# Six matmuls into a spare PSUM tile between the last output projection and the third piece of w4, in a decode kernel on one core

## The chip, the cores and the metric

The kernel runs on one core of one Trainium2 chip. The metric is the device time in microseconds. Executions of one kernel mostly agree within 0.3%; each comparison below is made on one chip, against executions of the kernel before in the same rounds. Times within a trace count from the start of its span.

In the profiles, PE is the engine for matmuls, PEld its weight loads, DVE and ACT are the vector and scalar engines, and SP is the engine that issues the loads; a "q" behind a name is that engine's sequencer. PSUM is the memory that matmuls write to. "Landing" is the moment at which a load has arrived. The granted clock is the share of its full clock that PE was given. Score matmuls are those of q k^T, PV matmuls those of p v; a V tile is the load of V that one head needs. Only some lines of each view are shown.

## The reference, cut to what matters

The reference adds two branches to its input: attention of one new token over the last 2048 entries of a K and V cache (4 batches, 32 query heads, 16 KV heads, head size 128), and a small MLP.

```
xn  = layernorm(x)                         # x: 4 x 1 x 576
q   = xn @ wq                              # 576 x 4096
p   = softmax(q k^T / sqrt(128))           # over the last 2048 positions
a   = (p v) @ wo                           # 4096 x 576
...                                        # layernorm; for S=1 the shifted part adds zero
h2  = gelu(layernorm(x1) @ w3) @ w4        # 576 x 4608, 4608 x 576
out = x + a + x1 + h2
```

Nearly all bytes are K and V (67 MB); w4 is 5.3 MB. All that is summed into the output is accumulated in PSUM, at the end in two tiles that are then added.

## The kernel before

The loads stand in one queue: K and V tiles in turn, wo in four parts, w3, and last w4 in six pieces. SP issues each when its buffer comes free. PE transposes and multiplies behind them. Only the tail matters here. `acc` and `acc_odd` are two PSUM tiles; their matmuls have 8 output rows each, in different column groups of the array, and two of them run side by side: in the trace of before the two of a pair start within 0.01 us of each other, and the pairs follow at 0.12 us. `mlp_out` multiplies rows of w4, `o_proj` rows of wo; a "row" in this text is one of the 36 blocks of 128 rows of w4.

```python
W4_PIECES = [0, 10, NFH, NF - 6, NF - 2, NF - 1, NF]     # 0, 10, 18, 30, 34, 35, 36

def load_w4():
    t = wp.tile([P, NF, D], BF16, tag="w", name="w4_sb")
    for lo, hi in zip(W4_PIECES, W4_PIECES[1:]):
        ...
        nc.sync.dma_start(out=t[:, lo:hi, :], in_=src[...])
...
def mlp_out(lo, hi):
    w4 = w_tiles["w4"]
    for i in range(lo, hi, 2):
        acc_matmuls([(gT[:, u, :], w4[:, u, :]) for u in range(i, min(i + 2, hi))])
...
mlp_out(*pieces[0])
o_turn(hl)                  # transposes, DVE sums, spreading: the last heads' attention
o_sum(hl)
o_spread(hl)
o_pick(hl)
mlp_out(*pieces[1])
o_proj(hl)                  # the last output projection, 16 matmuls
mlp_out(*pieces[2])         # the third piece of w4: rows 18 to 29
mlp_out(*pieces[3])
second.clear()              # from here all into acc
odd = const.tile([OR, CW], F32)
nc.scalar.activation(out=odd[:], in_=acc_odd[QD:QD + OR, :], func=ACT.Copy)
...
for lo, hi in pieces[4:]:   # the last two rows
    mlp_out(lo, hi)
fin = ...                   # acc + odd, to the output
```

## Time and profile before

| what | value |
|---|---|
| median of 3 executions, then of 6 | 211.7 us, 211.75 us (211.63 to 211.93) |
| span of the trace | 209.8 us |
| PE, DVE, ACT busy | 71%, 57%, 16% |
| DMA | 87.32 MB, of them 87.17 by the main queue; mean 416 GB/s |

These lines are from the page of before: the granted TensorE clock and the busy share of the DMA engines in 40 slices, in tenths, then the shares of the chain of waits by engine.

```profile
PEclk9999589696997556958999979997999985969999
DMA  8999999999999999999999999999999999999991
DMA 73%; PE 17%; DVE 7%; ACT 1%; issue 1%; SPq 0%; DVEq 0%
```

DMA is busy from end to end.

The next lines are the timeline of before in its tail: start, duration, engine, line, operation, what it writes and reads, shapes, count, and in brackets the idle time of the engine before it with what ended that.

```profile
203.96 0.29 PE L183 MATMUL acc<-wo_sb,op 128*8 128x288 bf16 x1
204.59 0.28 PE L183 MATMUL acc<-w_sb,gT 128*8 128x288 bf16 x1 [0.34 <-DMA w_sb<-in_B_w_dram]
...
206.55 0.65 PE L183 MATMUL acc<-w_sb,gT 128*8 128x288 bf16 x4
206.75 0.40 ACT L606 ACTIVATE odd<-acc_odd 8x288 f32<-8x288 f32 x1 [7.07 <-PE acc_odd L183]
...
207.72 0.36 SPq L614 DMA_DIRECT2D out_dram<-fin  x1
```

The projection's last matmul starts at 203.96. PE then waits 0.34 us for the third piece of w4, works without a gap to 207.2, and the output follows.

Last, from the view of one line's instructions, the issue of the third and of the sixth piece in before. "DMA to landing" is the time from issue to arrival.

```profile
L141 SPq DMA_DIRECT2D w_sb<-in_B_w_dram x1: 328/328/328, 169.9 to 169.9; - x1
DMA to landing us min/median/max: 34.6/34.6/34.6
...
L141 SPq DMA_DIRECT2D w_sb<-in_B_w_dram x1: 328/328/328, 184.5 to 184.5; - x1
DMA to landing us min/median/max: 22.1/22.1/22.1
```

The third piece lands at 169.9 + 34.6 = 204.5, the sixth at 184.5 + 22.1 = 206.6, which is 3.2 us before the end of the span.

### The profile page before, as it was taken

To read this page: it belongs to the slowest core of one execution; us is meant where nothing else is said; L and a number is where in the kernel's file an instruction comes from. 1 tells how busy PE (TensorE), PEld (TensorE's weight loads), DVE (VectorE), ACT (ScalarE), POOL (GpSimd) and SP (SyncE) were. 2 spreads that over 40 slices of the span, in tenths; PEclk is the share of its full clock that TensorE was granted. 3 is DMA by queue.
4 is the path that set the end of the run, shared out by engine and by line. 5 is a ranking of instruction groups with operands and counts; after the bars stand their busy time and mean duration, and the time that the engine had idled before them with its cause. 6 is when DMAs were issued, how large, how long until landed. Compare 5 with 4: busy or idle time off the path is not lost.

```text
span 209.8 us, 2403 instructions
## 1 busy us (share of the span) xinstructions
PE 149.1 (71%) x955; PEld 62.7 (30%) x955; DVE 120.4 (57%) x217; ACT 33.9 (16%) x64; POOL 2.8 (1%) x15
## 2 busy tenths in 40 slices
PE   0287496869691009659899599967994926989884
PEld 0133132223240003214364144332532401425353
DVE  3741899584840082825706878985399571771420
ACT  7602201020220000202102121120111110202300
POOL 4010000000000000000000000000000000000000
PEclk9999589696997556958999979997999985969999
DMA  8999999999999999999999999999999999999991
GB/s 301 400 419 431 434 428 419 439 428 425 445 429 427 423 431 425 449 419 431 440 422 434 434 409 444 434 428 423 444 414 437 418 450 419 434 428 421 434 409 69
DMA packets 6659, 87.32 MB, mean 416 GB/s; under 512 B 748, under 2 KB 1016, under 8 KB 1400
## 3 DMA queue, kind: packets, MB, share of 16 engines
q1 hardware_dynamic: 6640, 87.17, 97.5%
q8 instruction: 7, 0.11, 0.2%
q10 hardware_dynamic: 8, 0.00, 0.1%
q14 instruction: 4, 0.03, 0.0%
HBM read 87.17 MB, written 0.00 MB: 415 GB/s over the span
## 4 chain that ended last, share of the span: by engine, by line
DMA 73%; PE 17%; DVE 7%; ACT 1%; issue 1%; SPq 0%; DVEq 0%
DMA w_sb<-in_B_w_dram 33%; DMA vn<-in_A_v_cache_dram 24%; DMA wo_sb<-in_A_wo_dram 10%; DMA wq_sb<-in_A_wq_dram 6%; PE S L338 6%; DVE kt L225 4%; PE acc L183 3%; PE g_ps L456 2%; PE q_ps L285 2%; PE O L390 1%; PE oT L403 1%; DVE qz L317 1%; PE gT_ps L468 1%; DVE mx L344 1%; ACT q_sb L296 1%
## 5 line engine op out<-in xcount | busy, mean ns | idle before, releaser
L225 DVE STREAM_TRANSPOSE kt<-kn 128x1024 int32<-128x1024 int32 x64 | 76.5, 1216 | 12.4 <-DMA kn<-in_A_k_cache_dram 12.1
L338 PE MATMUL S<-kt,qz 128*128 128x512 bf16 x256 | 78.9, 437 | 3.1 <-DVE kt L225 3.1
L390 PE MATMUL O<-vn,PT 128*32 128x512 bf16 x256 | 27.2, 425 | 39.9 <-DMA vn<-in_A_v_cache_dram 38.1
L338 PEld LDWEIGHTS <-qz 128*128 128x128 bf16 x256 | 21.6, 103 | 41.1 <-issue 25.1
L366 ACT ACTIVATE E<-S 128x512 bf16<-128x512 f32 x16 | 9.6, 597 | 122.4 <-PE S L360 122.4
L390 PEld LDWEIGHTS <-PT 128*32 128x32 bf16 x256 | 7.2, 94 | 48.1 <-issue 29.6
L372 DVE STREAM_TRANSPOSE PT<-E 128x512 bf16<-128x512 bf16 x16 | 11.4, 710 | 15.3 <-ACT E L366 15.2
L397 ACT ACTIVATE O_sb<-O,rd 128x512 f32<-128x512 f32 x16 | 11.0, 686 | 15.8 <-issue 11.0
L356 DVE TENSOR_REDUCE nm<-mg 8x1 bf16<-8x16 f32 x16 | 2.4, 151 | 19.0 <-PE mg L351 19.0
L413 DVE TENSOR_REDUCE on<-oT 128x8 bf16<-128x128 f32 x16 | 4.5, 279 | 13.4 <-PE oT L403 13.4
L344 DVE TENSOR_REDUCE mx<-S 128x1 f32<-128x512 f32 x16 | 10.5, 657 | 1.3 <-PE S L338 1.3
L403 PE MATMUL oT<-ident_w,O_sb 128*128 128x128 f32 x64 | 11.2, 304 | 0.0
L403 PEld LDWEIGHTS oT<-ident_w,O_sb 128*128 128x128 f32 x64 | 9.1, 159 | 5.0 <-issue 3.2
L183 PE MATMUL acc<-wo_sb,op 128*8 128x288 bf16 x56 | 7.5, 286 | 0.0
L376 PEld LDWEIGHTS dn<-rs,same_j 128*128 128x128 f32 x32 | 5.8, 188 | 2.9 <-ACT E L366 0.7
L360 PE MATMUL S<-nm,j_row 8*128 8x512 bf16 x16 | 6.4, 402 | 0.0
L329 PE MATMUL S<-negbig,ohT 4*128 4x512 bf16 x16 | 6.2, 385 | 0.0
L183 PE MATMUL acc<-w_sb,gT 128*8 128x288 bf16 x38 | 5.1, 286 | 0.3 <-DMA w_sb<-in_B_w_dram 0.3
L183 PEld LDWEIGHTS <-op 128*8 128x8 bf16 x64 | 4.6, 87 | 2.5 <-issue 0.7
L351 PE MATMUL mg<-dm,sel_jb 128*8 128x16 bf16 x16 | 2.8, 174 | 3.6 <-DVE dm L346 3.5
L351 PEld LDWEIGHTS <-sel_jb 128*8 128x8 bf16 x16 | 1.3, 83 | 12.3 <-issue 5.6
L474 DVE COPY g_x<-gT_ps 128x64 f32<-128x64 f32 (+1 forms) x3 | 0.6, 193 | 7.7 <-PE gT_ps L468 7.7
(93 smaller groups left out, 84.6 us busy)
## 6 DMA issues: line engine op xcount, KB each, us to landing
kn<-in_A_k_cache_dram SPq DMA_DIRECT2D x16, 2048.0 KB, 22.0
vn<-in_A_v_cache_dram SPq DMA_DIRECT2D x16, 2048.0 KB, 24.4
wo_sb<-in_A_wo_dram SPq DMA_DIRECT2D x4, 1152.0 KB, 24.4
w_sb<-in_B_w_dram SPq DMA_DIRECT2D x1, 4608.0 KB, 34.0
wq_sb<-in_A_wq_dram SPq DMA_DIRECT2D x1, 4096.0 KB, 12.8
w_sb<-in_B_w_dram SPq DMA_DIRECT2D x1, 1728.0 KB, 34.6
w_sb<-in_B_w_dram SPq DMA_DIRECT2D x1, 1440.0 KB, 29.2
w_sb<-in_B_w_dram SPq DMA_DIRECT2D x2, 576.0 KB, 32.9
```

The source lines that it names most:

```text
L183: nc.tensor.matmul(out=to[q:q + OR, :], lhsT=lhsT[:, NI - 1 - i:NI - 1 - i + OR], rhs=rhs[:, i * CW:(i + 1) * CW], start=start, stop=False ...
L225: nc.vector.transpose(out=kt[:], in_=src)
L329: nc.tensor.matmul(out=S_ps[h][:].rearrange("p (c k) -> p c k", k=QD), lhsT=ohT[:], rhs=negbig[:].unsqueeze(1).to_broadcast([B, SC, QD]), ...
L338: nc.tensor.matmul(out=S_ps[h][:], lhsT=qz[:, z0:z0 + P], rhs=kt[:, ib, :, e:2 * QD:2].rearrange("p c k -> p (c k)"), start=False, stop=Fa ...
L344: nc.vector.reduce_max(out=mx[:], in_=S_ps[h][:], axis=AX.X)
L360: nc.tensor.matmul(out=S_ps[h][:], lhsT=j_row[:], rhs=st.pop(("nm", h))[:, 0:1].to_broadcast([NJ, NW]), start=False, stop=False, skip_grou ...
L366: nc.scalar.activation(out=E[h][:].rearrange("p c k -> p (c k)"), in_=S_ps.pop(h)[:], func=ACT.Exp, scale=scale, accum_out=rs[:])
L372: nc.vector.transpose(out=PT[h][:], in_=E.pop(h)[:])
L376: nc.tensor.matmul(out=dn[:], lhsT=same_j[:], rhs=st.pop(("rs", h))[:], start=True, stop=True)
L390: nc.tensor.matmul(out=O_ps[h][g * QD:(g + 1) * QD], lhsT=PT[h][:, c, :], rhs=vn[:, :, c, :], start=(s == 0), stop=False, skip_group_check ...
L397: nc.scalar.activation(out=O_sb[h][:], in_=O_ps.pop(h)[:], func=ACT.Copy, scale=st.pop(("rd", h))[:, 0:1])
L403: nc.tensor.transpose(out=oT[:, s, :], in_=o[:, s, :], identity=ident_w[:, s * NJ:s * NJ + P])
```

## The change

The name of the tile, `warm`, suggests the intent: to keep PE at work, and so its clock up, while it waits for the third piece. Nothing reads the tile.

```diff
     mlp_out(*pieces[1])
     o_proj(hl)
+    warm = ps_s.tile([P, NW], F32, tag="S", name="warm")
+    for _ in range(6):
+        nc.tensor.matmul(out=warm[0:OR, :], lhsT=gT[:, 0, 0:OR], rhs=w_tiles["w4"][:, 0, 0:NW], start=True, stop=True)
     mlp_out(*pieces[2])
     mlp_out(*pieces[3])
```

## The prediction

> **What bounds the kernel now.** DMA. The page shows the 16 DMA engines busy 0.9 in 38 of 40 slices, 416 GB/s over the span of 209.8 us; the chain of waits is 73% DMA. PE, 71% busy, has only a short tail after the last loads. The change touches this tail alone, so I read it from the timeline and the stretches after 199 us:
>
> - piece two of w4 and the last output projection keep PE in steady work; the projection's last pair starts at 203.96 and has streamed by about 204.1 (records run to 204.25);
> - PE then waits 0.34 us for DMA (the wait shown at PE for w_sb): the third piece of w4 lands at 204.55;
> - from 204.59 nothing waits: 16 pairs of 128x8 by 128x288 matmuls, 0.12 us a pair, to 206.55; four single ones to 207.20; then ACT's copy, DVE's copy and sum (0.41, 0.14, 0.43 us) and the output.
>
> So after 204.59 PE sets the end. Pieces four to six land before PE comes to them (DMA 0.53 busy in 205 to 206, 0.10 in 206 to 207).
>
> **Clock.** The intent is presumably to keep the clock up over that wait. But the stretches show a granted clock of 1.00 in every microsecond from 196 to 209. The Trainium skill ("TensorE: Matmul & The Clock Gate", section "HAM oscillation — how this bites in real kernels") warns of PE-idle gaps above about 3.4 us; here the gap is 0.34 us, and the trace shows no drop. There is nothing to win.
>
> **What is added.** Six matmuls of 128x8 by 128x512, all into the same eight PSUM rows, so one after another, and in the columns that acc's matmuls use next. Their operands and the spare S buffer are ready long before: no new wait. Four 128x512 score matmuls in this tail take 1.08 us, a single record 0.39 us, so one each (1.08-0.39)/3 = 0.23 us; the skill's same page (section "Back-to-back issue gap") gives N/2.4 + 2.5 ns = 0.216 us when warm, which agrees nearly. Six cost 1.3 to 1.4 us of PE. Their small weight loads hide. Nothing is removed; DMA order, DVE and ACT stay.
>
> **On the critical path.** The six run from about 204.1 to 205.4. Piece three's first matmul moves from 204.59 to 205.4: about 0.5 us of the six fits into the wait, 0.8 us does not. The rest of the chain moves with it, since nothing behind has slack. Net +0.8 us, 0.4%.
>
> **Predicted: 212.5 us**, 8 in 10 between 211.8 and 213.0. Faster by over 2%: 0.01; within 2%: 0.98; slower by over 2%: 0.01.
>
> **What the profile would show.** The six as 128x512 matmuls with records near 0.39 us, spaced 0.22; PE's wait for the third piece gone; its first matmul near 205.4; then the same 16 pairs at 0.12 us; PE's end near 208.0 rather than 207.2; the landings of w4 unchanged within scatter; clock 1.00 in both tails.
>
> **What would make it wrong.** (a) Without the profiler the third piece may land later relative to PE: the six hide, change 0 to 0.5 us. (b) It may land before the projection ends: the full 1.3 us shows. (c) If timed runs lose clock in the tail where the profiled one doesn't, the 16 pairs cost up to twice and the change could win 1 to 2 us. (d) The framework may order the spare tile or the read of w4 behind a later DMA: several tenths more. (e) Scatter between runs (0.3 us here) is near half the effect.

## The result, and the profile after

The median is 211.92 us (211.59 to 212.8, 6 executions), against 211.75 us before. The ratio is 1.0012, with a 95% interval of 0.9991 to 1.0033 (-0.2 to +0.7 us). Here and below, a ratio is the mean time of one kernel's runs over that of the other's of the same rounds, so it is not quite the ratio of the quoted medians. No difference is shown. The forecast of 0.8 us would be a ratio of 1.0038, just outside the interval.

The trace of after comes from the slowest of its six executions (212.8 us). These are lines of its timeline.

```profile
204.38 0.29 PE L183 MATMUL acc_odd<-wo_sb,op 128*8 128x288 bf16 x1
204.50 1.24 PE L604 MATMUL warm<-w_sb,gT 128*8 128x512 bf16 x5
205.39 0.41 PE L183 MATMUL acc_odd<-w_sb,gT 128*8 128x288 bf16 x2
205.58 0.38 PE L604 MATMUL warm<-w_sb,gT 128*8 128x512 bf16 x1
...
205.79 0.29 PE L183 MATMUL acc<-w_sb,gT 128*8 128x288 bf16 x1
...
208.93 0.36 SPq L617 DMA_DIRECT2D out_dram<-fin  x1
```

At first sight this is the prediction come true. The six are spaced (205.58 - 204.50)/5 = 0.216 us, PE's wait is gone, and the span grew by 1.2 us, to 211.0. But here are the issues of the third and the sixth piece in after:

```profile
L141 SPq DMA_DIRECT2D w_sb<-in_B_w_dram x1: 328/328/328, 170.4 to 170.4; - x1
DMA to landing us min/median/max: 35.0/35.0/35.0
...
L141 SPq DMA_DIRECT2D w_sb<-in_B_w_dram x1: 328/328/328, 185.0 to 185.0; - x1
DMA to landing us min/median/max: 22.5/22.5/22.5
```

The third piece landed at 205.4 in this execution, and the sixth at 207.5; both were at 204.5 and 206.6 in the trace of before. (The difference of these rounded times is 0.9 us; the first matmuls on the third piece, at 205.39 and 204.59, give 0.8.) Two matmuls of `acc_odd` on the new piece start at 205.39, before the sixth of the six at 205.58, though they stand behind it in the program: in this trace it is the first matmul into `acc`, in the column group that the six use, that comes only after all of them, at 205.79. So about 0.8 of the 1.2 us is late DMA in the slowest of the six executions, and only 205.8 - 205.4 = 0.4 us can be the six. Two single traces can't settle an effect of this size; the experiments had to.

### The profile page after: what moved, and what is told of

The parts are those of the page before. It is cut to its first block, busy times and chain, and to the rows that moved or that the text cites. A ratio compares the mean times of both kernels' runs of the same rounds, so it can differ in the third digit from the quotient of the medians.

```text
span 211.0 us, 2415 instructions
## 1 busy us (share of the span) xinstructions
PE 150.1 (71%) x961; PEld 62.8 (30%) x961; DVE 120.4 (57%) x217; ACT 33.9 (16%) x64; POOL 2.7 (1%) x15
## 4 chain that ended last, share of the span: by engine, by line
DMA 59%; PE 28%; DVE 9%; ACT 1%; issue 1%; SPq 0%; DVEq 0%
DMA vn<-in_A_v_cache_dram 36%; DMA w_sb<-in_B_w_dram 16%; PE S L338 10%; DMA wq_sb<-in_A_wq_dram 6%; PE acc L183 5%; DVE kt L225 4%; PE O L390 3%; PE oT L403 2%; PE g_ps L456 2%; PE q_ps L285 2%; DVE mx L344 1%; PE S L360 1%; DVE qz L317 1%; PE gT_ps L468 1%; DVE PT L372 1%
```

## The experiments

The theory of the prediction (A below) is that about 0.5 us of the six hides and 0.8 us shows, in every execution. B says that the wait is usually longer. C says that the clock falls in the tail and that the six prevent that. D was formed after the first four runs.

### Six again, 24, six in a later place, and a finer cut of w4

**e1_six** is the changed kernel once more.

> The changed kernel again, for more executions. Theory A (the six take 1.3 us of PE, 0.5 us of it falls into time in which PE would have waited for the third piece of w4, the rest moves the whole end): +0.8 us, ratio near 1.0037. Rival B (in executions that are not the one looked at, the third piece lands later against PE, so that the wait is about 1 us and most of the six fits into it): +0.2 to +0.3 us, ratio near 1.001. Rival C (the clock falls in the tail of some executions of before, and the six prevent that, which pays back part of their cost): an effect of 0.2 to 0.3 us, with a granted clock in the last 10 us below 1.00 in some trace of before.

Measured: 211.67 us against 211.65 us of before, ratio 0.9995 (0.9969 to 1.0022). The cost of the six is nothing, or at most half a microsecond: A's 0.8 us lies outside the interval (-0.7 to +0.5 us). The timeline of this execution:

```profile
202.34 0.29 PE L183 MATMUL acc_odd<-wo_sb,op 128*8 128x288 bf16 x1
202.46 1.46 PE L604 MATMUL warm<-w_sb,gT 128*8 128x512 bf16 x6
...
204.52 0.28 PE L183 MATMUL acc<-w_sb,gT 128*8 128x288 bf16 x1 [0.60 <-DMA w_sb<-in_B_w_dram]
```

The projection was over 1.6 us earlier than in the trace of before (202.34 against 203.96 for its last matmul), the third piece came at the same time, and all six fitted in with 0.60 us to spare.

**e2_24** has 24 in place of six:

```diff
-    for _ in range(6):
+    for _ in range(24):
```

> 24 matmuls in place of six. They take 24 times 0.207 us = 5.0 us of PE (spacing in the trace of the changed kernel: 204.50 to 205.58 for five, 0.216 us each, so 5.0 to 5.2). What the wait hides is a constant, so the rise tells its mean size: A: +4.6 us (0.5 us hidden). B: +4.0 to +4.2 us (1.0 us or more hidden). C: as A less what the clock gives; the same as B here, told apart by the granted clock.

Measured: 215.05 us, ratio 1.0158 (1.0126 to 1.0189), +3.4 us. The 24 take 24 x 0.216 = 5.2 us, so 1.8 us are hidden on average. That is B's side and not A's (+4.6); it lies below B's +4.0 to +4.2 too. The single executions range from 214.63 to 216.42.

**e3_late** moves the six behind the fourth piece, where PE has no wait:

```diff
     o_proj(hl)
     mlp_out(*pieces[2])
     mlp_out(*pieces[3])
+    warm = ps_s.tile([P, NW], F32, tag="S", name="warm")
+    for _ in range(6):
+        nc.tensor.matmul(out=warm[0:OR, :], ...)          # as in the change
```

> The six moved behind the fourth piece of w4, where PE has no wait and nothing can hide them. A, B: +1.3 us, all of the six (A: 0.5 us more than with the six in their first place, B: about 1.0 us more). C: +1.3 us as well, as the clock has no wait to fall in. If this also shows only 0.2 to 0.5 us, then the end of the kernel is not set by PE here and all three are wrong.

Measured: 212.94 us, ratio 1.0051 (1.0027 to 1.0075), +1.3 us between the medians (1.1 between the means, in which one execution of before at 213.3 weighs): the whole of the six. So they do cost 1.3 us where nothing hides them, and the end does hang on PE behind the third piece. Up to the third piece this kernel is the same as before, and its timeline shows there:

```profile
204.49 0.28 PE L183 MATMUL acc<-w_sb,gT 128*8 128x288 bf16 x1 [1.87 <-DMA w_sb<-in_B_w_dram]
```

The wait was 1.87 us, not 0.34.

**e4_split** puts useful work in the wait instead: the third piece is loaded in two halves.

```diff
-    W4_PIECES = [0, 10, NFH, NF - 6, NF - 2, NF - 1, NF]
+    W4_PIECES = [0, 10, NFH, NF - 12, NF - 6, NF - 2, NF - 1, NF]
...
     mlp_out(*pieces[3])
+    mlp_out(*pieces[4])
...
-    for lo, hi in pieces[4:]:
+    for lo, hi in pieces[5:]:
```

> No added matmuls; instead the third piece of w4 (12 rows) is loaded as two of six rows, so that PE has useful work in the time in which it waited. A: the wait of 0.34 us is filled, and the end comes up to 0.34 us earlier: -0.2 to -0.3 us. B: the wait is about 1 us, the first half fills 0.7 us of it: -0.5 to -0.8 us. C: less than A, and clock 1.00 in both. [...]

Measured: 211.77 us, ratio 0.9999 (0.9975 to 1.0023). No gain is shown. The interval, -0.5 to +0.5 us, is against B's 0.5 to 0.8 us; it can't rule out the 0.2 to 0.3 us of A, or C's less. The timeline shows why the full wait can't be won.

```profile
206.31 0.28 PE L183 MATMUL acc<-w_sb,gT 128*8 128x288 bf16 x1 [0.15 <-DMA w_sb<-in_B_w_dram]
```

PE has done both halves and now waits for the next piece, rows 30 to 33. The issue of the last piece in this trace:

```profile
L141 SPq DMA_DIRECT2D w_sb<-in_B_w_dram x1: 328/328/328, 189.8 to 189.8; - x1
DMA to landing us min/median/max: 17.2/17.2/17.2
```

It landed at 189.8 + 17.2 = 207.0 in this execution, 3.2 us before the end of its span (210.2), just as in before. So PE, freed from one wait, meets the last landings. In before two limits lie almost together: the third piece's landing plus PE's work (PE ends at 207.2), and the last landing plus what remains (206.6, with the last two matmuls from about 206.8).

### Where the length of the wait comes from

The traces so far fall into two kinds. From the first PV matmuls on the V tile that lands at about 184.5, to the start of the projection's last matmul, PE takes 19.4 us in the traces of before, after and e4_split, but 17.9 us in e1_six, e2_24 and e3_late. The unchanged kernel was then run under a label of its own, **e6_same**, and 12 matmuls in the place of the six, **e5_12** (`range(12)`).

> The kernel of before, unchanged, under a label of its own: ratio 1.000, to see the noise of this comparison. D: in its trace the wait for the third piece is either near 0.3 us with a half-clock stretch at 185 to 188, or near 1.9 us with a clock of 1.00 there, and the time is the same in either case. A: 0.3 us whatever the clock.

Measured: 211.69 us, ratio 1.000 (0.9987 to 1.0012). This trace is of the second kind. Its timeline:

```profile
202.34 0.29 PE L183 MATMUL acc<-wo_sb,op 128*8 128x288 bf16 x1
...
204.48 0.28 PE L183 MATMUL acc<-w_sb,gT 128*8 128x288 bf16 x1 [1.86 <-DMA w_sb<-in_B_w_dram]
```

It is the same kernel as in the first trace, and ends at the same time (span 209.7 against 209.8 us), yet PE waits 1.86 us and not 0.34. The view by stretches shows why, first of before, then of e6_same. The columns are busy times of each engine with counts, the granted clock, the DMA share and GB/s.

```profile
core 0: us, PE busy (x) PEld busy (x) DVE busy (x) ACT busy (x) POOL busy (x), PEclk, DMA share, GB/s
185.00:186.00 1.00, 1.00 (x3) 0.29 (x2) 1.00 (x2) 0.00 (x0) 0.00 (x0) 0.50 1.03 442
186.00:187.00 1.00, 1.00 (x7) 0.12 (x5) 0.59 (x3) 0.00 (x0) 0.00 (x0) 0.50 0.92 393
187.00:188.00 1.00, 1.00 (x7) 0.28 (x4) 1.00 (x1) 0.00 (x0) 0.00 (x0) 0.50 1.11 475
188.00:189.00 1.00, 1.00 (x7) 0.63 (x5) 0.14 (x1) 0.00 (x0) 0.00 (x0) 0.79 1.04 442
```

```profile
185.00:186.00 1.00, 1.00 (x9) 0.30 (x7) 0.96 (x3) 0.00 (x0) 0.00 (x0) 1.00 1.07 459
186.00:187.00 1.00, 1.00 (x8) 0.44 (x5) 1.00 (x3) 0.00 (x0) 0.00 (x0) 1.00 0.84 360
187.00:188.00 1.00, 1.00 (x9) 0.70 (x8) 1.00 (x2) 0.00 (x0) 0.00 (x0) 1.00 1.15 492
188.00:189.00 1.00, 1.00 (x10) 0.71 (x9) 0.23 (x2) 0.00 (x0) 0.00 (x0) 1.00 1.00 426
```

These are the V tile's first PV matmuls and the score matmuls behind them, again of before and then of e6_same.

```profile
184.54 0.40 PE L390 MATMUL O<-vn,PT 128*32 128x512 bf16 x4 [1.45 <-DMA vn<-in_A_v_cache_dram]
184.88 1.80 PE L338 MATMUL S<-kt,qz 128*128 128x512 bf16 x4
```

```profile
184.44 0.40 PE L390 MATMUL O<-vn,PT 128*32 128x512 bf16 x4 [0.91 <-DMA vn<-in_A_v_cache_dram]
184.77 1.08 PE L338 MATMUL S<-kt,qz 128*128 128x512 bf16 x4
```

In before the clock was 0.50 from 185.0 to 188.4; a group of four score matmuls took 1.80 us there, against 1.08 us in e6_same. PE was behind by about 1.5 us from then on. PE had time to spare, so the end of before doesn't show it. That is theory D. The traces without matmuls added further up agree: the three that take 19.4 us have a half clock that begins between 185.0 and 185.5, and the five that take 17.9 us (e1_six, e2_24, e3_late, e5_12, e6_same) have a clock of 1.00 there.

> Twelve matmuls, 2.6 us of PE. Theory D (from the six traces so far: the wait for the third piece has no fixed length; it is about 2.1 us where the clock stays at 1.00 after the V tile that lands at 184.5, and 0.3 us where a half-clock window of 3.4 us falls there and makes the chain to the output projection 1.5 us longer; the end of before is the same in both, as the landing decides): single executions between +0.5 us (full clock) and +2.2 us (half clock), median near +0.7. Theory A of the prediction (0.5 us hidden in every execution): +2.1 us in all of them.

Measured: 212.38 us, ratio 1.0032 (1.0020 to 1.0045), +0.7 us. A would have +2.1. The twelve take 2.6 us, so 1.9 us were hidden. The five executions lie between 212.10 and 212.71; none is near the +2.2 us that D gives an execution with the half clock.

Together: 6, 12 and 24 matmuls took 1.3, 2.6 and 5.2 us of PE and cost 0.0 to 0.2, 0.7 and 3.4 us (medians). The hidden part stops growing at 1.8 to 1.9 us, the length of the wait at full clock. (The intervals of the ratios leave 1.6 to 2.2 us for the twelve and 1.2 to 2.5 us for the 24; A's 0.5 us is outside both.) C has nothing for it: in before and e6_same the clock is 1.00 from 189 to the end of the span, with or without a long wait.

### Bringing the short wait about

If the half clock matters only by delaying PE, then seven matmuls (7 x 0.216 = 1.5 us) ahead of the first piece of w4 should do the same. **e9_delay** has them alone, **e10_delay_six** has them and the six of the change.

```diff
+    delay = ps_s.tile([P, NW], F32, tag="S", name="delay")
+    for _ in range(7):
+        nc.tensor.matmul(out=delay[0:OR, :], lhsT=gT[:, 0, 0:OR], rhs=qz[:, 0:NW], start=True, stop=True)
     mlp_out(*pieces[0])
```

> Before, with seven 128x512 matmuls (1.5 us of PE) ahead of the first piece of w4: they push the chain to the output projection back by what a half-clock window cost it in the trace first looked at (19.4 against 17.9 us). D: 1.5 of the wait of about 1.9 us is filled, the end is set by the landing as before: 0 to +0.3 us; the wait in the trace is 0.3 to 0.4 us, as in the first trace of before, at a clock of 1.00. A (wait always 0.3 us): +1.2 us.

> The same seven, and the six of the change. D: now the six meet the short wait that the first trace showed, 0.3 to 0.5 us of the 1.3 are hidden: +0.8 to +1.1 us over before, that is +0.8 over the seven alone, which is what the prediction gave the change. A: +2.5 us. If the sum is 0.3 or less, the end doesn't hang on the third piece in these executions and D falls.

Measured: the seven alone 211.64 us, ratio 0.9987 (0.9969 to 1.0005) to before, so they cost nothing that shows. With the six 212.38 us, ratio 1.0022 (1.0005 to 1.0039). Executions were close: 211.57 to 211.71 and 212.25 to 212.41. The six thus cost 212.38 - 211.64 = 0.74 us once the seven are there, near D's +0.8. Over before the medians differ by 0.56 us, less than the +0.8 to +1.1 that D had said: that part missed. The timeline of e9_delay, then of e10_delay_six:

```profile
204.01 0.29 PE L183 MATMUL acc_odd<-wo_sb,op 128*8 128x288 bf16 x1
204.68 0.28 PE L183 MATMUL acc<-w_sb,gT 128*8 128x288 bf16 x1 [0.38 <-DMA w_sb<-in_B_w_dram]
```

```profile
203.99 0.29 PE L183 MATMUL acc_odd<-wo_sb,op 128*8 128x288 bf16 x1
...
205.19 0.38 PE L607 MATMUL warm<-w_sb,gT 128*8 128x512 bf16 x1
205.41 0.29 PE L183 MATMUL acc<-w_sb,gT 128*8 128x288 bf16 x1
```

The wait is 0.38 us, as in the first trace of before, at a clock of 1.00 in the whole tail from 185. And 205.41 - 204.68 = 0.73 us is what the six move the third piece by. This is the arithmetic of the prediction, with its number, where its premise is made to hold.

### An attempt to prevent the half clock

Six matmuls more, placed where PE waits for the V tile that lands at 184.5, were to keep PE busy before the stretch in question.

```diff
+            if t == Hkv - 1 and s == 0:
+                early = ps_acc.tile([P, NW], F32, tag="g", name="early")
+                for _ in range(6):
+                    nc.tensor.matmul(out=early[0:OR, :], lhsT=gT[:, 0, 0:OR], rhs=qz[:, 0:NW], start=True, stop=True)
             if hv >= 0:
                 pv(hv, s)
```

> The changed kernel with six more matmuls of the same size, placed where PE waits for that V tile (the third last stage's first PV step), into the PSUM buffer that acc_odd takes later. D: if idleness of PE before the tile landed is what brings the half-clock window, the window at 185 to 188 is gone, the chain to the projection takes 17.9 us in every execution (from the tile's PV to the last projection matmul), and both sixes together cost 0 to 0.3 us, with less scatter than the changed kernel had (211.5 to 212.8). A: the early six cost up to 0.9 us on top of 0.8. If the window is still there in the trace, the idleness of that wait is not its cause.

> 24 matmuls in the place of the change, and the early six besides. D: all executions at full clock in the tail; the early six push the chain back by 0.4 to 1.0 us, so the hidden share falls from 2.1 to between 1.1 and 1.7: +3.5 to +4.1 us, with executions within 0.6 us of each other, where 24 alone ranged over 1.8 us. If the early six change nothing in the clock: the range stays.

Measured: with six in the change's place 211.81 us, ratio 1.0007 (0.9994 to 1.0020), within what D said of the time; the chain took 18.2 us in the trace, not 17.9. With 24 there 215.41 us, ratio 1.0190 (1.0156 to 1.0225): the median of +3.75 us is within D's range, but the executions run from 214.77 to 217.19, a wider range than without the early six. D's expectation of small scatter missed. Both traces show a clock of 1.00 from 180 on, but neither is one of the longer executions (spans of 210.0 and 213.5 us, which belong to times of about 211.8 and 215.3). The two slowest of the 24 (216.91 and 217.19 us) have a mean clock of 0.865 over the span, three others 0.879 or 0.880. One half-clock window of 3.4 us costs 0.5 x 3.4 / 213 = 0.008, so they had about two more; where, no trace tells. So the early six are not shown to be a remedy, and which executions lose the clock stays open.

## Why the prediction was right or wrong

The measured 211.92 us lies within the range forecast, 211.8 to 213.0, but only by 0.12 us, and that is luck: repeated in e1_six, the same kernel had 211.67 us, below the range. Its main number, +0.8 us, is not what was measured (+0.17 us between the medians, and +0.02 us when repeated).

- **Cost of the six: right.** Forecast 1.3 to 1.4 us; their spacing is 0.216 us, and e3_late shows 1.3 us where nothing hides them.
- **No new waits, nothing removed: right.** They started 0.12 us after the projection's last pair, the spacing of matmuls that wait for nothing.
- **Clock: the conclusion right, the reading too narrow.** The clock was 1.00 from 196 to 209, as said, and stays so over a wait of 1.87 us in e3_late; there was nothing for the six to win. But the clock that mattered had been lost before, at 185 to 188.
- **"About 0.5 us of the six fits into the wait, 0.8 us does not": this step failed.** It took the 0.34 us of one trace for a property of the kernel, and so forecast a cost that the medians don't show. Where the clock holds, the wait is 1.86 us (e6_same), and all six fit. Where the half clock falls at 185 to 188, the wait is short, and the six show; e10_delay_six reproduces that case with 0.74 us.
- **"What would make it wrong", (a): the direction right, the cause not.** The prediction said that without the profiler the piece may land later relative to PE. It does so in other executions, with the profiler as well, because PE comes earlier.
- **Pieces four to six have landed in time: right, but by little.** The sixth lands at 206.6, and its matmuls start at about 206.8. The prediction took that for room; the trace of e4_split shows that there is almost none.

Shown: the two lengths of wait in one kernel with one end, the hidden 1.8 to 1.9 us by the doses of 12 and 24, and the 0.7 us with the wait made short. Read from traces only: that the half clock is what delays PE (three traces against five); no run switched the clock alone. Argued only: that the spread of after's own six executions (211.59 to 212.8) comes from this. Its one trace mixes a half clock with late landings, and before, without the six, also has executions of 212.92 and 213.3 us in later rounds. No kernel of this study is shown to beat either of the two.

## What to carry to other kernels

A wait read from one trace is one draw: before hiding work in it, read it in several executions, and ask what sets both of its ends (here a DMA landing on one side, and a chain on PE that is 1.5 us longer at a half clock on the other). Time that goes unseen because an engine has slack is still a change of that slack, so look at the clock well upstream of the place that is changed. And before filling a wait with useful work, read which landing comes next: here the last landings were so close behind that no gain showed.

## What the Trainium skill lacked or had wrong

- "TensorE: Matmul & The Clock Gate", section "HAM oscillation — how this bites in real kernels", advises against PE-idle gaps above about 3.4 us. Much less was enough here. In the first trace of before, PE was busy 1.97 us of the window of 3.41 us ahead of the half clock, with no gap above 1.45 us (first block below, stretches cut where the clock changed). With 2.04 us in e2_24 the clock held (second block). Over the windows of twelve traces, aligned to the changes of the clock and counted from the first clock record on (17 to 20 us), every full-clock window with less than 1.58 us busy was followed by half clock, and none with more than 2.21 us; between these both occur. From half to full it took at least 2.66 us busy, and a window with 2.79 us stayed at half. The page also tells, in "A second HAM failure mode: psum-queue depth-cycling", of a clock lost to short but frequent idle times; it has no such shares.

```profile
181.59:185.01 3.42, 1.97 (x18) 0.96 (x19) 3.35 (x7) 0.69 (x1) 0.00 (x0) 1.00 0.97 417
185.01:188.42 3.41, 3.41 (x12) 0.83 (x11) 2.72 (x4) 0.00 (x0) 0.00 (x0) 0.50 1.02 437
```

```profile
182.16:185.57 3.41, 2.04 (x18) 0.95 (x19) 3.34 (x7) 0.69 (x1) 0.00 (x0) 1.00 1.02 437
185.57:188.99 3.42, 3.42 (x24) 1.71 (x23) 2.89 (x5) 0.00 (x0) 0.00 (x0) 1.00 0.98 422
```

- The same page, section "What's actually happening", has the window free-running and 3413 ns long, and counts what its phase does as a matter of the warm-up at a kernel's start. The length agrees (0.50 from 185.01 to 188.42). But the clock differs between executions of one kernel late in it too: the end of a chain on PE near 203 us came 1.5 us later with the half clock. Whether the phase decides which execution has it is not shown.
- The same page, section "Back-to-back issue gap", gives N/2.4 + 2.5 ns as the gap of an isolated matmul, and says that in a stream of pairs of weight load and matmul this over-counts: about 131 ns each for N = 512. Here the six have 512 columns, 8 output rows and a weight load each, and their spacing of 0.216 us is that of the formula, not 131 ns. The 0.23 us that the prediction worked out from score matmuls was too long for the six.
